# Loading the activation row of a decode-attention kernel: element-wise loads, or one row spread over the partitions by TensorE

## Chip, cores, metric

One core of one Trainium2 chip. The metric is the device time of one execution in microseconds (us), smaller is better. Before the change: 1961.84 us, the median of 3 runs (1961.54 to 1963.42).

## The reference, cut to what matters

Two independent attention blocks, A and B, each with one query token for each of 2 batch entries, 32 heads of 192, and a cache of 8192 positions. All arrays are bf16.

```python
q = (x @ wq).reshape(B, 1, 32, 192)            # x: [2, 1, 640], wq: [640, 6144]
scores = einsum("bhqd,bhkd->bhqk", q, k_cache) * 192 ** -0.5
p = softmax(scores)
o = einsum("bhqk,bhkd->bhqd", p, v_cache)      # k_cache, v_cache: [2, 32, 8192, 192]
out = o.reshape(B, 1, 6144) @ wo               # wo: [6144, 640]
```

Per block the two caches are 201 MB each and x is 2.5 KB. The outputs of A and B are concatenated.

## The kernel before

The work is cut into 128 units (block, head, batch entry). Each loads 3 MB of k and 3 MB of v through SyncE's DMA queue into two buffers each (`NK = NV = 2`). DVE multiplies k by q, ACT and DVE sum the products, ACT takes the exponential, and PE multiplies p with v. q is made on PE: the x of a batch entry must stand as `xbc`, 128x128 weights for each of the 5 chunks of 128, with the same value across all columns. Then q comes out equal on all 128 partitions.

```python
xT  = [[sb(f"xT{k}_{b}",  [128, DC], BF16) ...]]       # DC = 5
xbc = [[sb(f"xbc{k}_{b}", [128, DC, 128], BF16) ...]]

def sp_x(blk, b):                                      # one element per descriptor
    src = blocks[blk]["x"][b, 0, :].rearrange("(c j) -> j c", j=128)
    def fn(eng):
        with nc.allow_non_contiguous_dma(reason="tiny x transpose load"):
            return eng.dma_start(xT[blk][b][:], src).then_inc(xsem[blk], 16)
    return fn

def xbc_copy(blk, b):
    return lambda eng: eng.tensor_copy(xbc[blk][b][:], xT[blk][b][:].unsqueeze(2).broadcast_to([128, DC, 128]))
...
for b in range(B):
    S_sp.add(sp_x(0, b))                               # block A, ahead of everything
S_sp.add(sp_wq(0, 0) if WQSPLIT else sp_wq(0))
# ... then k0 (two parts), wq's second part, block B's two x loads, k1, v0, k2, v1, ...
for blk in range(1, NBLK):
    for b in range(B):
        S_pool.add(xbc_copy(blk, b), waits=[("x", blk)], ...)   # block B on POOL
for b in range(B):
    S_dve.add(xbc_copy(0, b), waits=[("x", 0)], ...)            # block A on DVE
```

k0, k1, ... and v0, v1, ... are the k and v of units 0, 1, .... SyncE issues k of unit u when DVE has finished its last product with k of unit u-2, and v of unit u when PE has finished with v of unit u-2. POOL runs a maximum over partitions for every unit, without which neither the exponential nor PE's product with v can start.

## Time and profile before

| | |
|---|---|
| span of the profiled execution | 1961.8 us |
| bytes moved | 837 MB, 430 to 433 GB/s in most slices |
| SyncE's DMA queue, share of 16 engines' span | 99.7% |
| busy: DVE, PE, ACT | 84%, 57%, 46% |

From the page of the profile of before: the mean rate in 40 equal slices of the span, the DMA packets, the queue of SyncE (q1: packets, MB, share), and the chain of work that ended last, by engine.

```profile
GB/s 371 429 430 431 432 430 433 431 430 433 431 433 433 429 432 433 431 433 431 432 430 431 432 430 433 431 432 428 435 432 431 432 430 433 431 432 431 432 432 299
DMA packets 56476, 837.12 MB, mean 427 GB/s; under 512 B 7416, under 2 KB 18304, under 8 KB 23680
...
q1 hardware_dynamic: 56432, 836.79, 99.7%
...
DMA 72%; PE 22%; DVE 5%; issue 1%; SPq 0%; ACT 0%; DVEq 0%
```

All slices but the first and the last run at the same rate: the kernel is bound by the DMA stream, and what can be won lies in its head (371 GB/s in the first 49 us) and its tail (299 GB/s in the last). The Trainium skill, "DMA: Bandwidth & Descriptors", § Specifications, gives a fabric ceiling of 435 GB/s; the 428 to 435 of this trace's full slices agree with it as a ceiling.

The head, from the timeline of before (start us, us, engine, line, operation, out<-in, count; in brackets the engine's idle time's end and what ended it). SPq lines are DMA issues.

```profile
0.73 0.97 SPq L249 DMA_DIRECT2D xT<-in_A_x_dram  x2
...
1.75 0.52 SPq L242 DMA_DIRECT2D wqs<-in_A_wq_dram  x1
...
2.31 1.00 SPq L242 DMA_DIRECT2D kb<-in_A_k_cache_dram  x2
3.35 0.43 SPq L242 DMA_DIRECT2D wqs<-in_A_wq_dram  x1
3.83 7.34 SPq L249 DMA_DIRECT2D xT<-in_B_x_dram  x2
4.10 1.55 DVE L289 COPY xbc<-xT 128x640 bf16<-128x640 bf16 x2 [4.10 <-DMA xT<-in_A_x_dram]
...
6.07 1.78 PE L387 MATMUL qps<-wqs,xbc 128*128 128x384 bf16 x5 [6.07 <-DMA wqs<-in_A_wq_dram]
...
11.21 0.53 SPq L242 DMA_DIRECT2D kb<-in_A_k_cache_dram  x1
...
11.79 2.27 SPq L242 DMA_DIRECT2D vb<-in_A_v_cache_dram  x1
...
16.21 6.17 POOL L289 COPY xbc<-xT 128x640 bf16<-128x640 bf16 x2 [10.97 <-DMA xT<-in_B_x_dram]
18.84 0.33 SPq L242 DMA_DIRECT2D kb<-in_A_k_cache_dram  x1
```

x for block A takes the first 0.97 us of SyncE. q waits for wq, and the first k product on DVE for q. Block B's two loads then hold SyncE for 7.34 us (the second alone for 6.64, while each of block A's took 0.41 or 0.51). What holds SyncE there the trace does not show; DMA rings that were still full are the likely reading.

A second place, from the windows of before (stretch in us, its length, busy us of PE, PEld, DVE, ACT and POOL with the number of instructions, granted PE clock, DMA share, GB/s):

```profile
14.00:33.00 19.00, 2.29 (x7) 0.88 (x8) 18.72 (x9) 7.24 (x43) 12.05 (x4) 1.00 1.04 382
33.00:60.00 27.00, 11.54 (x51) 5.68 (x50) 24.32 (x14) 12.24 (x69) 2.68 (x4) 0.68 1.01 429
```

From 14 to 33 us the engines are fully busy and still move 382 GB/s instead of 429 or more. The packet records of the trace say why: in k1 and v0 a 24 KB packet takes 1020 ns, from k2 on it takes 912. The text below calls this the slow phase.

### The profile page before, as it was taken

What the parts mean: (1) busy time and instruction counts of PE and PEld (TensorE: products, weight loads), DVE (VectorE), ACT (ScalarE), POOL (GpSimd) and SP (SyncE); (2) the same over time, 40 slices, a digit from 0 to 9 for tenths busy, and PEclk for the clock granted to TensorE, in tenths of its full rate; (3) what the DMA queues carried; (4) which work ended last, traced back from release to release, by engine and by line L of the source; (5) the groups of instructions that cost most, each with busy time, mean ns of one, the idle gap of its engine ahead of it and who ended that gap; (6) DMA issues with size and microseconds to landing.
All of it is one profiled execution on the core that took longest, in us unless ns stands there. A gap on an engine that the chain in (4) does not pass through costs nothing.

```text
span 1961.8 us, 18371 instructions
## 1 busy us (share of the span) xinstructions
PE 1115.6 (57%) x5004; PEld 590.1 (30%) x5004; DVE 1656.0 (84%) x962; ACT 903.0 (46%) x4743; POOL 172.8 (9%) x270
## 2 busy tenths in 40 slices
PE   2445546655566555655655556556564665556657
PEld 1222223332333223322333333223332332223324
DVE  7889898888888888898888988888888888888884
ACT  4445444445444444454444444444445444544442
POOL 3013030000001000000000000000000000000000
PEclk9777777777777777777777777777777777777778
DMA  9999999999999999999999999999999999999997
GB/s 371 429 430 431 432 430 433 431 430 433 431 433 433 429 432 433 431 433 431 432 430 431 432 430 433 431 432 428 435 432 431 432 430 433 431 432 431 432 432 299
DMA packets 56476, 837.12 MB, mean 427 GB/s; under 512 B 7416, under 2 KB 18304, under 8 KB 23680
## 3 DMA queue, kind: packets, MB, share of 16 engines
q1 hardware_dynamic: 56432, 836.79, 99.7%
q8 instruction: 12, 0.20, 0.0%
q14 instruction: 16, 0.13, 0.0%
q10 hardware_dynamic: 16, 0.01, 0.0%
HBM read 836.77 MB, written 0.01 MB: 427 GB/s over the span
## 4 chain that ended last, share of the span: by engine, by line
DMA 72%; PE 22%; DVE 5%; issue 1%; SPq 0%; ACT 0%; DVEq 0%
DMA vb<-in_B_v_cache_dram 35%; DMA vb<-in_A_v_cache_dram 29%; PE ops L405 22%; DMA kb<-in_A_k_cache_dram 8%; DVE prodD L309 3%; DVE prodD L316 1%; DVE prodA L305 0%; DVE sc L320 0%; PE oTps L414 0%; PE oTps L425 0%; PE outps L441 0%; SPq L242 0%; SPq L249 0%; DVE mp L312 0%; ACT oTzL L359 0%
## 5 line engine op out<-in xcount | busy, mean ns | idle before, releaser
L405 PE MATMUL ops<-vb,pb 128*33 128x384 bf16 x4032 | 939.9, 408 | 774.1 <-DMA vb<-in_B_v_cache_dram 387.5
L405 PEld LDWEIGHTS ops<-vb,pb 128*33 128x33 bf16 x4032 | 473.4, 120 | 1231.5 <-DMA vb<-in_B_v_cache_dram 405.8
L327 ACT ACTIVATE prodA<-prodA 128x192 bf16<-128x192 bf16 x2048 | 709.0, 350 | 117.0 <-DVE prodA L305 116.8
L309 DVE TENSOR_TENSOR prodD<-kb,qbc 128x9216 bf16<-128x9216 bf16 x128 | 633.7, 4951 | 3.6 <-DMA kb<-in_A_k_cache_dram 3.6
L316 DVE TENSOR_TENSOR prodD<-prodD 128x4608 bf16<-128x4608 bf16 (+2 forms) x384 | 599.0, 1560 | 13.3
L305 DVE TENSOR_TENSOR prodA<-kb,qbc 128x3072 bf16<-128x3072 bf16 x128 | 225.2, 1759 | 238.9 <-DMA kb<-in_B_k_cache_dram 126.9
L327 ACT ACTIVATION_READ_ACCUMULATOR prodA<-prodA 128x1 f32 x2048 | 386.9, 189 | 0.0
L331 ACT ACTIVATE nb<-mg 128x1 f32<-128x1 f32 x128 | 25.9, 203 | 737.0 <-POOL mg L292 737.0
L292 POOL PARTITION_ALL_REDUCE mg<-mp x128 | 56.3, 440 | 1637.5 <-DVE mp L312 1637.5
L320 DVE TENSOR_REDUCE sc<-prodD 128x48 f32<-128x1152 bf16 x128 | 173.2, 1353 | 4.4
L296 POOL PARTITION_ALL_REDUCE lall<-rs x128 | 105.6, 825 | 114.7 <-ACT pb L334 114.7
L387 PE MATMUL qps<-wqs,xbc 128*128 (+1 forms) x320 | 67.9, 347 | 53.4 <-ACT qbc L365 42.4
L414 PEld LDWEIGHTS oTps<-ones,o_sb 33*128 33x128 f32 x372 | 67.1, 258 | 9.8 <-issue 9.8
L414 PE MATMUL oTps<-ones,o_sb 33*128 33x1 f32 x372 | 69.8, 311 | 0.0
L341 ACT ACTIVATE o_sb<-ops 1x384 f32<-1x384 f32 x63 | 29.9, 475 | 86.0 <-PE oTps L414 75.5
L365 ACT ACTIVATE qbc<-qps 128x384 bf16<-128x384 f32 x64 | 31.3, 488 | 77.4 <-PE qps L387 76.7
L334 ACT ACTIVATE pb<-sc,nb 128x64 bf16<-128x64 f32 x128 | 52.2, 408 | 16.6 <-ACT nb L331 8.3
L387 PEld LDWEIGHTS qps<-wqs,xbc 128*128 128x128 bf16 x320 | 27.2, 101 | 88.7 <-ACT qbc L365 44.3
L312 DVE TENSOR_REDUCE mp<-sc 128x1 f32<-128x64 f32 x128 | 28.2, 220 | 13.7 <-issue 4.7
L441 PE MATMUL outps<-wos,oTz 128*4 (+1 forms) x186 | 31.1, 304 | 15.1 <-ACT oTz L359 15.1
L342 ACT ACTIVATE o_sb<-ops 1x384 f32<-1x384 f32 x63 | 30.3, 481 | 0.7
L334 ACT ACTIVATION_READ_ACCUMULATOR pb<-sc,nb 128x1 f32 x128 | 23.8, 186 | 0.0
(27 smaller groups left out, 78.1 us busy)
## 6 DMA issues: line engine op xcount, KB each, us to landing
vb<-in_A_v_cache_dram SPq DMA_DIRECT2D x64, 3072.0 KB, 22.2
kb<-in_B_k_cache_dram SPq DMA_DIRECT2D x64, 3072.0 KB, 23.0
kb<-in_A_k_cache_dram SPq DMA_DIRECT2D x63, 3072.0 KB, 22.5
vb<-in_B_v_cache_dram SPq DMA_DIRECT2D x60, 3072.0 KB, 22.8
wos<-in_A_wo_dram SPq DMA_DIRECT2D x8, 960.0 KB, 26.8
wqs<-in_B_wq_dram SPq DMA_DIRECT2D x8, 960.0 KB, 24.5
wos<-in_B_wo_dram SPq DMA_DIRECT2D x8, 960.0 KB, 26.8
wqs<-in_A_wq_dram SPq DMA_DIRECT2D x7, 960.0 KB, 24.5
```

The costliest lines, as they stand in the source:

```text
L292: return lambda eng: eng.partition_all_reduce(mg[u % 2][:], mp[u % 2][:], 128, bass.bass_isa.ReduceOp.max)
L296: return lambda eng: eng.partition_all_reduce(lall[g % 2][:, b:b + 1], rs[u % 2][:], 128, bass.bass_isa.ReduceOp.add)
L305: return lambda eng: eng.tensor_tensor(prodA[u % 2][:, 0:na, :], kb[u % NK][:, 0:na, :], qb_bc(u, na), ALU.mult)
L309: return lambda eng: eng.tensor_tensor(prodD[:, 0:T - na, :], kb[u % NK][:, na:T, :], qb_bc(u, T - na), ALU.mult)
L316: return lambda eng: eng.tensor_tensor(prodD[:, 0:nd, 0:w], prodD[:, 0:nd, 0:w], prodD[:, 0:nd, w:2 * w], ALU.add)
L320: return lambda eng: eng.tensor_reduce(sc[u % 2][:, na:T], prodD[:, 0:T - na, 0:24], AXL.X, ALU.add)
L327: return lambda eng: eng.activation(prodA[u % 2][:, t, :], prodA[u % 2][:, t, :], ACTF.Identity, accum_out=sc[u % 2][:, t:t + 1])
L334: return lambda eng: eng.activation(pb[u % NPB][:, :, ::32], sc[u % 2][:].rearrange("p (j a) -> p j a", a=2), ACTF.Exp, bias=nb[u % 2][:], ...
L365: return lambda eng: eng.activation(qbc[qg % 4][:], qps[:, 0:QW].rearrange("p (a d) -> p a d", a=2), ACTF.Identity)
L387: ins = eng.matmul(qps[:, 0:QW], xbc[blk][b][:, c, :], wqs[:, slot, c, off].rearrange("p a n -> p (a n)") if slot is not w % 2 else wqs[:, ...
L405: ins = eng.matmul(ops[(u // B) % 2][0:33, b, 0:QW], pb[u % NPB][:, j, :], vv[:, j, :], start=(j == 0), stop=(j == T // 2 - 1))
L414: ins = eng.matmul(oTps[:, 2 * i + b:2 * i + b + 1], o_sb[:, b, :, :].rearrange("p s (r i) -> p i (s r)", i=3)[:, i, :], ones33[:], start= ...
```

## The change

The intent: take the element-wise loads away. x of a block is loaded as one contiguous row on one partition, through ScalarE's (ACT's) queue, so that SyncE's queue starts with wq. PE spreads it: a chunk of the row is the weights, with one row and 128 columns, a row of ones is the moving operand, and the product is x of that chunk on 128 partitions, equal across 128 columns. DVE or ACT evicts it from PSUM into `xbc`.

```diff
+        xrow = [sb(f"xrow{k}", [1, B, DC, 128], BF16) for k in range(NBLK)]
+        one1 = sb("one1", [1, 128], BF16)
...
+        def ld_x(blk):
+            src = blocks[blk]["x"].rearrange("b o (c j) -> o b c j", j=128)
+            return dma(xrow[blk][:], src, xsem[blk])
...
+        def pe_x(blk, b):
+            def fn(eng):
+                for c in range(DC):
+                    ins = eng.matmul(xps(b)[:, c, :], xrow[blk][0:1, b, c, :], one1[:], start=True, stop=True)
+                return ins
+            return fn
+        def act_x(blk, b):
+            return lambda eng: eng.activation(xbc[blk][b][:], xps(b), ACTF.Identity)
+        def dve_x(blk, b):
+            return lambda eng: eng.tensor_copy(xbc[blk][b][:], xps(b))
...
-        for b in range(B):
-            S_sp.add(sp_x(0, b))
         S_sp.add(sp_wq(0, 0) if WQSPLIT else sp_wq(0))
...
-                    for blk in range(1, NBLK):
-                        for b in range(B):
-                            S_sp.add(sp_x(blk, b))
...
+        for blk in range(NBLK):
+            S_act.add(ld_x(blk))
+        for b in range(B):
+            S_pe.add(pe_x(0, b), waits=[("x", 0), ("one1",)], sig=("xp", 0, b))
+        S_dve.add(dve_x(0, 0), waits=[("xp", 0, 0)], sig=("xbc", 0, 0))
...
+        S_act.add(act_x(0, 1), waits=[("xp", 0, 1)], sig=("xbc", 0, 1))
...      # block B: the same on PE and ACT, behind the first two q's; POOL's copies are gone
```

## The prediction

> **What bounds the kernel now.** The DMA engines. The page's slices show DMA at 9 tenths in all but the last and 430 to 433 GB/s in most; the queue table gives SyncE's queue 99.7%. 836.8 MB at 431 GB/s is about 1941 us, so only some 20 us of the 1961.8 us span is head and tail. DVE (84% busy), PE (57%) and ACT (46%) have slack. The chain of waits is 72% DMA. SyncE waits for free buffers (988 us on PE, 821 on DVE) while one or two 3 MB transfers are still queued: after 5 us no stretch shows starved DMA.
>
> So only what changes the start of the bulk stream, or the packets in it, can move the end. x occurs only in the first 23 us.
>
> **What the change removes.**
> 1. Block A's two element-wise loads head SyncE's queue: 0.97 us of issue (timeline), so wq's first part is issued at 1.75 instead of 0.73. In the packet records their 1280 two-byte packets run from 2.56 to 4.51 us; wq's first comes at 3.99. The Trainium skill, "DMA: Bandwidth & Descriptors", § Rules for kernel authors, says that a non-contiguous last dimension lowers to one descriptor per element; the trace agrees (640 two-byte packets per load). Without them wq should move from about 2.5 us: 1.4 to 1.5 us earlier, and with it k0, the first q and everything behind.
> 2. Block B's two loads hold SyncE from 3.8 to 11.2 us; no loss by itself, as the rings are full. Their 1280 packets run from 14.8 to 16.1 us and depress the stream (334, 322, 397, 246 GB/s in the four windows from 12 to 16 us, against about 424): 0.95 us short, of which 0.2 to 0.3 is wq's short rows, which stay. Gain about 0.7 us.
> 3. POOL's two copies (6.17 us) and DVE's two (1.55 us): off the DMA path.
>
> **What it adds.** Two row loads on ACT's queue (5 KB), 20 matmuls of 128 columns, three ACT evictions and one DVE eviction of 128x640. From the q matmul (327 ns for 384 columns) I estimate 0.11 us for 128 columns, 0.6 us per five; from the 384-column ACT eviction (0.49 us), 0.7 to 0.8 us for 640. Row issued at 0.73, landing about 3; the copies for q ready at 4.6 and 5.2, close to wq's new landing (4.6). Block B's part runs near 8 to 10 us and delays ACT's first accumulations by about 1 us; ACT is idle from 16.3 to 28 us, so it costs nothing.
>
> **On the critical path.** Items 1 and 2: 2.1 to 2.4 us. A second possible gain: k1 and v0 (15 to 33 us) ran at 1020 ns per 24 KB packet (393 GB/s); later ones at 912. The slow phase starts where block B's packets interleave. If they cause it, another 1.6 us goes; I give that 35 to 40%.
>
> **Predicted:** 1959.0 us (-0.14%), 8 in 10 within 1956.8 to 1961.0. Faster by over 2%: 0.5%; within 2%: 99%; slower by over 2%: 0.5%.
>
> **What would show it.** Timeline: wq's first issue near 0.7; first q matmul at 4.7 to 5.0 instead of 6.07; k1's and v0's issues near 4 instead of 11.2 and 11.8; k2's issue 1.3 to 1.5 us before 18.84. No window from 12 to 16 us below 330 GB/s. DMA view: 2560 fewer packets below 512 B. Whether 15 to 33 us still shows 393 GB/s decides the second gain. Later transfers all 2 to 4 us earlier, at the same rate; tail unchanged.
>
> **What would make it wrong.** The row landing so late that q comes after 6.07: DMA would still hide it, as k2 is needed only at 31.8. A packet phase that leaves the stream slow for longer. A tail whose order changes. Run-to-run spread is 1.9 us, almost the effect.

## The result

1958.7 us, the median of 4 runs (1957.39 to 1959.1); before, in the same rounds, 1961.69 us (1960.63 to 1963.42). The ratio is 0.9983, 95% interval 0.9965 to 1.0000: the same at the 2% mark, some 3 us quicker. Ratios here are the mean time of one kernel's fast runs over that of the other's of the same rounds, so not quite the ratio of the medians.

The same parts of the page, after:

```profile
GB/s 407 432 433 426 434 431 433 432 431 434 431 432 433 431 432 432 433 432 431 432 430 431 430 433 433 431 432 428 434 432 431 433 432 432 434 431 431 434 430 304
DMA packets 53857, 837.12 MB, mean 428 GB/s; under 512 B 4795, under 2 KB 15683, under 8 KB 21061
...
q1 hardware_dynamic: 53808, 836.78, 99.8%
...
DMA 70%; PE 23%; DVE 5%; issue 1%; ACT 0%; SPq 0%; DVEq 0%; POOL 0%
```

2621 fewer packets below 512 B (2560 of them the two-byte ones), and the first slice at 407 GB/s instead of 371. All other slices are as they were. The timeline of after:

```profile
0.73 0.41 SPq L243 DMA_DIRECT2D wqs<-in_A_wq_dram  x1
0.73 0.54 ACTq L243 DMA_DIRECT2D xrow<-in_A_x_dram  x1
...
1.19 0.99 SPq L243 DMA_DIRECT2D kb<-in_A_k_cache_dram  x2
1.31 0.23 ACTq L243 DMA_DIRECT2D xrow<-in_B_x_dram  x1
...
2.12 1.24 PE L291 MATMUL ops<-one,xrow 1*128 1x128 bf16 x10 [2.12 <-DMA xrow<-in_A_x_dram]
2.22 0.43 SPq L243 DMA_DIRECT2D wqs<-in_A_wq_dram  x1
2.70 0.60 SPq L243 DMA_DIRECT2D kb<-in_A_k_cache_dram  x1
...
2.87 0.82 DVE L299 CAST xbc<-ops 128x640 bf16<-128x640 f32 x1 [1.89 <-PE ops L291]
...
3.33 0.44 SPq L243 DMA_DIRECT2D vb<-in_A_v_cache_dram  x1
3.40 0.70 ACT L296 ACTIVATE xbc<-ops 128x640 bf16<-128x640 f32 x1
...
4.42 1.78 PE L397 MATMUL qps<-wqs,xbc 128*128 128x384 bf16 x5 [1.05 <-DMA wqs<-in_A_wq_dram]
...
17.14 0.33 SPq L243 DMA_DIRECT2D kb<-in_A_k_cache_dram  x1
```

wq is issued at 0.73 us, and its first packet moves at 1.80 us instead of 3.21 (packet records). x's row has landed by 2.12, PE takes 1.24 us for the ten matmuls of both batch entries, and `xbc` is ready at 3.69 and 4.10, before wq lands (4.42). q starts 1.65 us earlier and k2 is issued 1.70 us earlier. The same windows of after:

```profile
14.00:33.00 19.00, 6.18 (x22) 2.65 (x20) 18.69 (x10) 8.60 (x50) 5.88 (x2) 1.00 1.01 435
33.00:60.00 27.00, 11.54 (x54) 5.69 (x52) 26.31 (x15) 12.84 (x71) 7.22 (x4) 0.68 1.01 428
```

There is no slow phase: 435 GB/s where before had 382. By the packet records the transfers of after start earlier than those of before by 2.2 us (k1), 3.3 (v0), 4.1 (k2), 4.4 (k3), and this 4.3 to 4.5 us then stays to the last transfers (the very last packets are 4.95 us apart). The two profiled spans differ by 4.95 us, but the medians by only 3.0. So the pair of profiles holds something that the typical pair of runs does not. The experiments separate it.

### The profile page after: what moved, and what is told of

Read it like the earlier page. It is cut to its first block, busy times and chain, and to the rows that moved or that the text cites. A ratio compares the mean times of both kernels' runs of the same rounds, so it can differ in the third digit from the quotient of the medians.

```text
span 1956.9 us, 18439 instructions
## 1 busy us (share of the span) xinstructions
PE 1124.6 (57%) x5024; PEld 594.0 (30%) x5024; DVE 1654.6 (85%) x962; ACT 906.1 (46%) x4746; POOL 187.3 (10%) x268
## 4 chain that ended last, share of the span: by engine, by line
DMA 70%; PE 23%; DVE 5%; issue 1%; ACT 0%; SPq 0%; DVEq 0%; POOL 0%
DMA vb<-in_B_v_cache_dram 35%; DMA vb<-in_A_v_cache_dram 29%; PE ops L415 23%; DMA kb<-in_A_k_cache_dram 6%; DVE prodD L319 3%; DVE prodD L326 1%; DVE prodA L315 0%; DVE sc L330 0%; PE oTps L424 0%; PE oTps L435 0%; SPq L243 0%; PE outps L451 0%; PE qps L397 0%; DVE mp L322 0%; ACT oTzL L369 0%
## 5 line engine op out<-in xcount | busy, mean ns | idle before, releaser
L306 POOL PARTITION_ALL_REDUCE lall<-rs x128 | 124.6, 974 | 114.1 <-ACT pb L344 114.1
```

The costliest lines, as they stand in the source:

```text
L306: return lambda eng: eng.partition_all_reduce(lall[g % 2][:, b:b + 1], rs[u % 2][:], 128, bass.bass_isa.ReduceOp.add)
```

## The experiments

Four batches, on chips named 9, 8, 8 and 0. The middle of the quick executions of before was the same within 0.1 us in all four batches (1960.2 us), so times of different batches are compared by their quick groups (a quick group is the runs within about 1 us of the kernel's fastest; its median is given). All outputs were correct. Theory 1: the packets of the element-wise loads and their issue cost the time, and block B's also set off the slow phase. Rival: the slow phase is a chance of one execution and not the change's. A second rival for the gain: the place in SyncE's queue, not the packets.

### The two kernels again

No edit.

> The kernel before, unchanged, a second time. Theory 1 (block B's 1280 two-byte packets cause the slow phase): k1 and v0, 14.4 to 32 us, again take 1020 ns per 24 KB packet, 380 to 393 GB/s. Rival (the slow phase is a chance of one execution): it may be missing, and the third 3 MB transfer then starts 1.5 to 2 us earlier than in the first profile. Both: ratio to before 1.000 within 0.001.

> The kernel after, unchanged, a second time. Theory 1: no slow phase, 912 ns per packet from k1 on; ratio 0.9985, 2.5 to 4.5 us faster. Rival: the slow phase may turn up here, and the ratio then stands at 0.9985 to 0.9992.

> The kernel before, unchanged, a third profile. So far 2 of 2 profiles of before show 1020 ns packets for k1 and v0, 0 of 4 of the others. If the slow phase belongs to before in every execution, it is here again, and every time of before contains it. If it comes and goes, its times fall into groups about 2 us apart (near 1960.1, 1962 and 1963.5 us), and a profile whose time is near 1960.1 has no 1020 ns packets and ends its PV tail at full clock.

Before again: 1960.13, 1962.09, 1963.23, 1963.49, 1963.85 and 1975.9 us. After again: 1957.01, 1957.09, 1957.11, 1957.12, 1957.16 and 1959.01. Before a third time: 1960.06, 1961.73, 1962.45, 1966.0, 1970.14 and 1972.09. No run is over 1.5% above the fastest of its kernel. The ten executions of after (1957.01 to 1959.10) are all below the fastest of the 58 of before (1959.95), so that after is quicker does not hang on which runs are compared. Both new profiles of before have the slow phase. In the third, whose execution took 1966.0 us, it reaches into seven transfers; its last packet of 1020 ns starts at 71.6 us. Windows of before, third profile:

```profile
14.00:33.00 19.00, 2.21 (x7) 0.88 (x8) 18.72 (x9) 7.15 (x42) 12.01 (x4) 1.00 1.05 383
33.00:60.00 27.00, 11.94 (x47) 5.51 (x45) 21.83 (x14) 9.76 (x54) 1.48 (x4) 0.71 1.01 388
60.00:75.00 15.00, 11.64 (x56) 6.02 (x54) 9.93 (x7) 5.44 (x30) 0.74 (x2) 0.84 1.00 393
```

The rate stays at 383 to 393 GB/s over all three stretches. By the packet records the stream of the three profiles of before ends 4.5, 4.5 and 8.3 us behind that of after again; take off the 2.5 us that all four loads cost without a slow phase (below), and the slow phase cost 2.0, 2.0 and 5.8 us. (The packets agree: 256, 271 and 822 of them took 1020 ns, and 108 ns more for each on 16 engines makes 1.7, 1.8 and 5.5 us.) The medians beside these runs scatter for the same kernel (1960.27, 1961.77), and the means too (ratios 0.9994 and 1.0011 of before to itself; 0.9954 with an interval of 0.9896 to 1.0013 for after). So one number per kernel says little here.

A second source of spread is at the end, where DMA is done and PE works off the last units. Chain of work that ended last, PE's products for the last two units, before:

```profile
1941.99 6.98 PE ops L405 x32
...
1949.88 5.31 PE ops L405 x32
```

After, first profile:

```profile
1937.04 6.99 PE ops L415 x32
...
1944.93 5.31 PE ops L415 x32
```

After again:

```profile
1937.17 5.31 PE ops L415 x32
...
1943.38 5.31 PE ops L415 x32
```

The same 32 matmuls take 6.98, 6.99 or 5.31 us. The windows there show the reason; the granted clock is the third figure from the end, before the DMA share and GB/s. After, first profile, and then after again:

```profile
1937.00:1942.00 5.00, 5.00 (x22) 2.60 (x22) 0.00 (x0) 1.25 (x4) 0.00 (x0) 0.66 0.99 410
```

```profile
1937.00:1942.00 5.00, 5.00 (x32) 3.05 (x33) 0.00 (x0) 1.25 (x4) 0.00 (x0) 1.00 1.00 414
```

PE is busy for all of the 5 us in both, but with a granted clock of 0.66 in the one and 1.00 in the other. In windows of 1 us the clock of the first is 0.5 from about 1937.4 to 1940.8. The Trainium skill, "TensorE: Matmul & The Clock Gate", § Part 1: The HAM clock gate, says that the gate passes half the pulses after an idle window of about 3.4 us, and that the windows run freely, not in step with the kernel. The trace agrees only in part. An earlier half-clock stretch of the same profile (1920.3 to 1923.8 us) does follow 3.6 us without PE work, its half-clock stretches from 1900 us on to the tail last 3.4 or 6.8 us, and where such stretches start differs from execution to execution. But the stretch on the tail follows 3.4 us in which PE was busy throughout, and since 1923.8 us PE had never been idle for more than 0.93 us. What sets it off is thus open. It costs 1.7 us when it falls on this tail, in either kernel: of the 14 profiles five have it (the first of before, the first of after, and of the runs below both probes, late pairs and element-wise loads on ACT's queue). The two profiles of after, whose streams agree within 0.2 us, differ by 1.55 us in span. A half-clock tail would also explain the untraced 1959.0 among the 1957.1 of after; it is no part of the change.

### Each half of the change alone

Block A's row with block B's loads left as they were (POOL copies them, as before), and the reverse:

```diff
 # rowA_elemB
-            S_act.add(ld_x(blk))          # for both blocks
+        S_act.add(ld_x(0))
+                        for b in range(B):
+                            S_sp.add(sp_x(blk, b))        # block B, where it was
+            S_pool.add(xbc_copy(1, b), waits=[("x", 1)], sig=("xbc", 1, b))
 # elemA_rowB
+            S_sp.add(sp_x(0, b))                          # block A, ahead of wq
+            S_dve.add(xbc_copy(0, b), waits=[("x", 0)], sig=("xbc", 0, b))
-            S_pe.add(pe_x(0, b), ...)
...      # and the rest of block A's row path
```

> Block A's part of the change alone; block B's loads stay element-wise on SyncE's queue with POOL's copies. Theory 1: the first wq issue at 0.73, k1's first packet 1.4 us earlier than before, but the slow phase stays; gain 1.2 to 1.6 us (ratio 0.9993). Rival (slow phase by chance, or set off by block A's packets): no slow phase, gain 3 us or more (0.9984).

> Block B's part alone; block A's loads stay element-wise at the head of SyncE's queue. Theory 1: stream starts as late as before (first q matmul near 6.1), no slow phase; gain 0.8 us from the packets and about 2 us from the slow phase, 2.5 to 3 us in all (0.9986). Rival (slow phase not from block B's packets): gain 0.8 us (0.9996), slow phase may still be seen.

| | quick group (runs in it) | others | stream against after again: k1, k2, end |
|---|---|---|---|
| before, same rounds | 1960.17 (6) | 1961.74 to 1988.42 | |
| rowA_elemB | 1958.24 (4) | 1959.86, 1959.89 | +0.5, +1.0, +1.0 |
| elemA_rowB | 1958.89 (5) | 1960.62 | +1.6, +1.6, +1.8 |
| after again | 1957.11 (5) | 1959.01 | 0 |

From the quick groups, block A's loads cost 1958.89 - 1957.11 = 1.78 us and block B's 1958.24 - 1957.11 = 1.13 us. The sum, 2.9 us, leaves almost nothing of the 3.06 us between the quick groups of before and after. In the stream, the block A part is there at k1 and stays. Timeline of elemA_rowB:

```profile
0.72 1.00 SPq L251 DMA_DIRECT2D xT<-in_A_x_dram  x2
1.77 0.52 SPq L244 DMA_DIRECT2D wqs<-in_A_wq_dram  x1
```

wq goes out at 1.77 us, as before. Neither profile has the slow phase, and no execution of either kernel is more than 1.9 us above its fastest, which the tail's clock (1.7 us) can account for; a slow phase of 2.0 us would look nearly the same in these times. So theory 1 fell in one point, as far as two profiles go (this one and the early probe below): block B's packets alone need not set off the slow phase.

### The packets without their use

After, with element-wise loads into tiles that nobody reads: block B's two at their old place, or all four at their old places.

```diff
+        def dum(i):                       # as sp_x, into xdum[i], semaphore dsem[i]
 # a_probe_early
                         S_sp.add(sp_wq(0, 1))
+                    for i in range(2):
+                        S_sp.add(dum(i))
 # a_probe_both: also ahead of wq
+        for i in range(2):
+            S_sp.add(dum(i))
```

> The kernel after, plus block B's two element-wise loads into tiles that nobody reads, at their old place in SyncE's queue. If their packets and issue alone cost the time: k1 0.5 us and k2 about 1.0 us later than after, 1.0 us slower (1958.1), as with block A's row alone. If POOL's copies or the waiting for x cost it: same as after (1957.1).

> The kernel after, plus all four element-wise loads of before into tiles that nobody reads, at their old places in SyncE's queue. If the 2560 packets and their issue are what the change removed: stream as in before (k1 2.0 us later than after), and, if both pairs together set off the slow phase (3 of 3 profiles of before, 0 of 7 of the others), packets of 1020 ns again; 1960 to 1966 us. If the x path (POOL and DVE copies) mattered: nearer to 1958.

Early probe: 1958.12 to 1958.6 us in four runs, 1959.83 and 1960.17 in two; the stream was 0.6 us late at k1 and 1.1 from k2 to its end. Dead loads cost what block B's real ones cost, about 1.2 us, so POOL's copies and the wait for x were free. Both probes: 1959.77, 1959.9, 1961.49, 1961.58, 1962.51 and 1977.11 us. Its quick group is within 0.4 us of that of before (1960.16 in the same rounds) although x takes the new path; so the loads are nearly all that the change is worth. The profile (the run of 1961.49, span 1959.7 us) has no slow phase, and its stream ends 2.5 us behind after again. But 1977.11 us is a long execution as only before had had it.

### The place in the queue

Rows from SyncE's queue, and, the other way round, before with its element-wise loads on ACT's queue:

```diff
 # a_row_sp (from after)
+        S_sp.add(ld_x(0))                 # ahead of wq
         S_sp.add(sp_wq(0, 0) if WQSPLIT else sp_wq(0))
 ...
+                        S_sp.add(ld_x(blk))   # block B, behind wq's second part
-            S_act.add(ld_x(blk))
 # elem_actq (from before)
-            S_sp.add(sp_x(0, b))  ...  -  S_sp.add(sp_x(blk, b))
+        for blk in range(NBLK):
+            for b in range(B):
+                S_act.add(sp_x(blk, b))
```

> The kernel after with its two row loads on SyncE's queue, at the places that the element-wise loads had. If only the packets mattered: same as after. If the place ahead of wq costs its issue time: wq's issue 0.3 to 0.6 us later than after, and the stream and the end by as much (1957.5 to 1957.7); no slow phase.

> The kernel before with its four element-wise loads issued from ACT's queue instead of SyncE's, no TensorE part. If the place in SyncE's queue is the whole cost: stream as early as in after, 3 us faster than before (1957.1). If the 2560 packets cost by themselves (9 ns each on 16 engines is 1.4 us): first wq packet near 1.8 us, but k2 1.4 to 2 us later than after, 1958.5 to 1959.2.

Rows on SyncE's queue: 1957.4 to 1958.0 us in four runs and 1959.15 and 1959.28. Timeline:

```profile
0.72 0.33 SPq L243 DMA_DIRECT2D xrow<-in_A_x_dram  x1
1.11 0.41 SPq L243 DMA_DIRECT2D wqs<-in_A_wq_dram  x1
```

The row costs 0.33 us of issue, and the whole stream is 0.31 us late. That is all that ACT's queue gives to this change. The one row instead of 640 elements is the main part.

Element-wise loads on ACT's queue: 1978.22 to 1980.93 us in all six runs, ratio 1.0086 (1.0061 to 1.0112): the same at the 2% mark, but clear of noise some 20 us slower where 1 to 3 us quicker was expected by both theories. wq did start at 1.82 us. What went wrong shows in the waits up to 60 us (engine and line waited for what: us, times, longest):

```profile
POOL xbc L289 <- DMA xT<-in_B_x_dram: 48.2, 1, 48.2
...
PE ops L405 <- ACT pb L334: 33.2, 1, 33.2
ACT nb L331 <- POOL mg L292: 28.8, 1, 28.8
```

in what SyncE's queue waited for up to 80 us:

```profile
SPq L242 <- DVE prodD L309: 37.9, 3, 21.3
SPq L242 <- PE ops L405: 24.4, 1, 24.4
```

and in the windows:

```profile
30.00:45.00 15.00, 0.00 (x0) 0.00 (x0) 14.28 (x9) 0.00 (x0) 0.00 (x0) 1.00 1.01 431
45.00:58.00 13.00, 1.94 (x7) 0.94 (x8) 0.00 (x0) 2.64 (x16) 2.11 (x4) 1.00 0.64 258
58.00:75.00 17.00, 5.65 (x27) 2.88 (x25) 13.21 (x9) 9.70 (x56) 6.01 (x3) 0.78 0.62 250
```

On SyncE's queue block B's 1280 two-byte packets pass in 1.3 us. On a queue of their own they were still moving at 52.9 us (packet records), and block A's landed only at 14.6. The Trainium skill, "DMA: Bandwidth & Descriptors", § Queues, rings and completion order, says that a DMA engine goes round between the queues with work, a packet at a time. That fits: where large packets stand ready, the counts of the two kinds are equal (96 and 96 from 8 to 12 us, 66 and 66 from 16 to 20), so for each small packet a large one of the bulk queue passes, 0.7 to 0.9 us each. (A packet of the page holds several descriptors; whether the two kinds take turns one by one or in groups these counts do not show.) What a delay without waiting engines would cost was not tried. Here POOL's copies stand in POOL's program ahead of the maximum for unit 0. POOL's first copy waited 48.2 us for block B's x, ACT 28.8 for POOL, PE behind ACT, and SyncE 24.4 us for a v buffer; only then did the DMA engines run dry (258 and 250 GB/s). So the queue alone is no gain, and with element-wise loads it is a trap; the row does not suffer from it here: it has landed by 2.12 us, when the bulk stream has only just begun (1.80).

### Is it the place in time?

Two pairs of dead element-wise loads in the steady state, and then three pairs near the end.

```diff
+                if u in (20, 60):             # a_probe_three: (116, 118, 120)
+                    S_sp.add(dum(...)); S_sp.add(dum(...))
```

> The kernel after, plus two pairs of element-wise loads in the steady state, behind k20 and k60. If a pair costs what it does at the start: 0.5 to 1.1 us each, 1.0 to 2.2 us together (1958.1 to 1959.3). If such a pair sets off the slow phase wherever it stands: 1020 ns packets right behind them. If a pair in a full queue is hidden: 1957.1.

> The kernel after, plus three pairs of element-wise loads behind k116, k118 and k120 (near 1690, 1720 and 1750 us), so that one profile shows three trials. The two late pairs gave 1959.6 to 2049.6 us from run to run, and the one profile of them fell in a quick execution. If such pairs switch the stream into the slow phase by chance: the profile shows 912 ns packets up to one of the pairs and 1020 ns packets from there to the next pair or the end, and times spread from 1960 to about 1987 us. If the lost 70 to 90 us came from something else (a stall behind SyncE, a chip disturbance): all packets 912 ns, and times within 1960 to 1963 us.

Late pairs: 1959.6 and 1960.49 us, and 2031.01, 2047.65, 2049.43 and 2049.63 (the four are over 1.5% above the fastest; the granted clock was 0.716 to 0.724 in them). The profile fell on 1960.49 us: all transfers at 912 ns, the first pair delaying the stream by 0.9 us and the second by another 1.9. A pair is thus not hidden by a full queue. The four long executions were not traced, and nothing is concluded from them but that they came.

Three pairs: 1960.09, 1960.22, 1960.41, 1963.48 and 1965.21 us. The profile (1960.22 us) again shows 912 ns everywhere and 3.1 to 3.6 us of delay behind the three pairs, 1.0 to 1.2 us each. It was meant to catch the start of a slow phase, and it didn't: inconclusive on that.

### k0 ahead of wq

```diff
                     S_sp.add(sp_k(u, 0), waits=[key("d1b", u - NK)])
+                    S_sp.add(sp_wq(0, 0) if WQSPLIT else sp_wq(0))
...
-        S_sp.add(sp_wq(0, 0) if WQSPLIT else sp_wq(0))   # was ahead of k0
```

> The kernel after with k0's first part ahead of wq in SyncE's queue. If the 1.05 us from wq's issue to its first packet grows with its 640 short rows: k0's first packet at 1.3 to 1.6 us and the whole stream 0.2 to 0.5 us earlier than after (1956.7). If it is a fixed latency: no gain (1957.1). The first q comes about 1.8 us later; that should cost nothing, as the second k buffer and two v buffers are still loading.

1957.56 to 1957.96 us in five runs, 1959.15 in one; stream 0.2 to 0.4 us behind after again. The first packet moved at 1.72 us instead of 1.80. The time from issue to first packet is 1.07 us for 640 short rows and 0.99 for 128 long ones. It is nearly all latency and hardly a matter of the count, and there was nothing to win. No version tried beats the kernel after.

### All executions together

| kernels | executions | more than 2.4 us above the quick group | longest |
|---|---|---|---|
| before and its copies | 58 | 22 | 2025.59 |
| one early pair of element-wise loads (three kernels) | 18 | 0 | 1960.62 |
| rows only (after, its copy, rows on SyncE, k0 first) | 22 | 0 | 1959.28 |
| two or three pairs, unread (both probes, late pairs, three pairs) | 17 | 8 | 2049.63 |

For before, 2.4 us is counted from 1960.0; for the others from the kernel's own fastest. The tail's clock can add 1.7 us, so 2.4 and more needs another cause. The mark does not find every slow phase: the second profile of before has one, and its execution took 1962.09 us. Over all of them, the 58 executions of before have a median of 1961.9 us and a mean of 1965.1, the 10 of after 1957.3 and 1957.8. The six executions with element-wise loads on ACT's queue, long for the reason shown, are left out.

## Why the prediction was right

- **Time.** 1959.0 predicted, 1958.7 measured, inside 1956.8 to 1961.0. That it is so close is partly luck. The loads without a slow phase were worth 2.5 to 2.9 us, not 2.1 to 2.4; the weighted share of the second gain (35 to 40% of 1.6 us, so 0.6) made up for it. And the median of four runs falls on executions like the profiled one, whose tail had the half clock: over all ten of after it is 1957.3.
- **Bound by DMA; only head or packets count: right.** The offset that the stream gets in the first 35 us is the same 1850 us later (4.4 us in the profiles of the first pair).
- **Item 1, block A's loads: right, a little small.** 1.4 to 1.5 us predicted; 1.8 us from the quick groups, 1.6 in the stream. wq's first packet came 1.41 us earlier, as said. The rest fits with block A's last packets running between wq's first ones (3.21 to 3.73 us): wq's 640 packets started within 2.49 us instead of 2.19 (2.34 in after again). k2 was issued 1.70 us earlier, where 1.3 to 1.5 was expected.
- **Item 2, block B's loads: right in kind, too small.** 0.7 us predicted; 1.1 us measured with the real loads and about 1.2 with dead ones. I had read the loss off four windows alone; it goes on behind them: the early probe's stream was 0.6 us late at k1 and 1.1 at v0.
- **Item 3, off the path: right.** Dead loads cost what real ones did.
- **What it adds: hidden, as predicted**, with one term too large. The row landed by 2.12 us, not about 3. The ten matmuls took 1.24 us (1.2 predicted), the evictions 0.70 and 0.82 us (0.7 to 0.8). So q started at 4.42 us, before the predicted 4.7 to 5.0, bound by wq's landing alone.
- **The slow phase: half right.** It left with the change, in 2 of 2 profiles of after. But it isn't a fixed 1.6 us. It was in 3 of 3 profiles of before, with 2.0, 2.0 and 5.8 us, and by the times it is absent or shorter in the 19 of 58 executions near 1960 (none of those was traced). Block B's packets alone, which I had suspected, did not bring it.
- **Tail unchanged: right.** In the first pair both kernels had the half clock there (6.98 and 6.99 us for the same 32 matmuls); the last packets of the two streams are 4.95 us apart, as are the spans. From execution to execution the tail moves by 1.7 us with the clock.
- **A slip that didn't matter.** The packet times in the prediction are 0.78 us too late: I set the records' zero wrongly against the span. Block A's packets ran from 1.78 to 3.73 us, block B's from 14.0 to 15.3. Their differences, which the sum used, hold.

What stays open: what switches the stream from 912 to 1020 ns per packet and what ends it. That long executions come with element-wise loads is well supported (22 of 58 against 0 of 22); that two pairs are needed rests on 0 of 18 with one early pair (8 of 17 with two or three unread ones), and why is not known. That a long execution is long by a slow phase is shown for one of them only, the 1966.0 us of the third profile. No profile caught a switch outside of before, and the executions of 1970 us and more were not traced.

## What to carry to other kernels

In a kernel bound by the DMA stream, two-byte loads in the stream's queue are paid in stream time wherever they were tried, 0.9 to 1.9 us per 1280 elements here, and a full queue does not hide them; load a contiguous row and let an idle engine spread it. Moving small loads to a second queue saves only their issue (0.3 us here) and, if they consist of many packets, can delay their landing by tens of us beside bulk packets; look for what stands behind them in the waiting engine's program. When a change is smaller than the spread, take several profiles of both kernels and compare groups of runs, not one pair: here one pair said 4.95 us and the quick groups 3.1.

## What the Trainium skill lacked or had wrong

- "DMA: Bandwidth & Descriptors", § Latency and other measured facts, gives about 600 ns to the first byte of a DMA that SyncE or ACT issues (HWDGE, descriptors made in hardware), and does not say from which moment. Here the first packet came 1.0 to 1.1 us after the issue began (0.73 to 1.72, 1.80 and 1.82 us), for 128 rows of 6 KB as for 640 of 768 B; from the issue's end (1.11 and 1.14 us) it is 0.6 to 0.7 us.
- The same page, § Issuing engines are not separate DMA queues, says that a second issuing engine only saves issue time. It can also cost: block B's 1280 small packets took to 52.9 us on ACT's queue beside bulk packets, and 1.3 us on the bulk queue itself; as POOL stood waiting for them, the kernel lost 20 us.
- No page has the slow phase: 24 KB packets at 1020 instead of 912 ns (383 instead of 431 GB/s) for 16 to 56 us, in the three profiles of before.
- No page has the cost of an element-wise load inside a bulk stream: 0.9 to 1.9 us for 1280 elements (2.5 KB), mostly 1.0 to 1.2.
- "TensorE: Matmul & The Clock Gate", § Part 1: The HAM clock gate, gives an idle window of about 3.4 us as what brings the half clock. The half clock on the tail (1937.4 to 1940.8 us in the first profile of after) followed 3.4 us of unbroken PE work. It costs 1.7 us, most of the 2.1 us between the fastest and the slowest execution of after.
